# Experts' first products by one level of Strassen's algorithm (Winograd's form), in three passes of 768 tokens

## The chip, the cores and the metric

One core of one Trainium2 chip runs the kernel. The metric is device time in microseconds for one execution. TensorE (PE) multiplies matrices, VectorE (DVE) and ScalarE (ACT) work element by element, GpSimd (POOL) does almost nothing here, and SyncE (SP) issues the transfers between memory (HBM) and the on-chip buffer (SBUF). TensorE's results go to PSUM, eight banks of 512 float32 columns by 128 partitions.

## What is computed

```python
kv = einsum('bhsd,bhse->bhde', k, v); o = einsum('bhsd,bhde->bhse', q, kv)
x  = o / sqrt(mean(o*o, -1) + 1e-6) * g_norm      # 4 x 576 = 2304 tokens of 512
h  = x @ w_in;  x = (h * clip(h + 3, 0, 6) / 6) @ w_out          # first layer, 512 -> 2048 -> 512
p  = domain_probs / (domain_probs.sum(-1, keepdims=True) + 1e-9)
for e in range(4):                                               # second layer, 4 experts
    out += p[:, e:e+1] * (maximum(x @ w1[e], 0) @ w2[e])         # 512 -> 1024 -> 512
```

## The kernel before, in words

A float32 product runs as three passes in TensorE's float32r type: an operand is split into hi (rounded to float32r) and lo (the rest), and hi*hi + hi*lo + lo*hi is summed in PSUM. ScalarE makes hi, VectorE lo.

The 2304 tokens lie in blocks of 512 (four, and one of 256: `BLK`). Hidden features are worked on in feature tiles of 128. The first layer's 16 feature tiles are cut into four units (`UNITS1`), and each expert is a unit of 8. An item (u, t, f) is a feature tile f of unit u for token block t, and `items` runs over units, in them over blocks, in them over feature tiles. `ff_in` (L345 to L367) makes an item's hidden features: 12 products (4 tiles of d by 3 passes, L352 to L354) into one of two PSUM banks, then for an expert a ReLU on ScalarE (`gH`, L364) and lo on VectorE (`gL`, L365). `ff_out` (L369) multiplies them by the second matrix, three items later (`LAG`), into up to six banks: 12 products of the block's width in the first layer, and for an expert 3 products of 512 columns per token tile of 128 (L385). `ff_end` takes a block's sums out of PSUM after a unit's last feature tile: the first layer adds them to `acc` and at its end makes hi and lo of the second layer's input (`xH`, `xL`, L403, L404); an expert scales them by the token's probability and adds (L416, L418), and the last expert's are stored (L420).

`step` writes an item's products and, beside them, a few steps of weight conversion (`pull`, `convert`): float32 weights of the experts are split by L175 (hi) and L177 (lo), from blocks loaded by L126 and L130. All weights of the experts are loaded and split once. Instructions stand on each engine in an order that a scheduler settles when the kernel is built; each engine then runs its own in that order and waits at semaphores.

## Time and profile before

| | us |
|---|---|
| three timed executions | 1274.44, 1274.55 (median), 1275.44 |
| profiled execution, first to last instruction (its span) | 1272.9 |
| median above that span | 1.65 |
| TensorE busy in the span | 1257.5 |
| VectorE busy, ScalarE busy | 500.9, 354.7 |

The profiled execution has no time of its own in the results, only its span; the median of the timed executions stands for it, and 1.65 us lie outside the span. Busy time is the union of an engine's instructions. Products on TensorE overlap, so their mean duration is longer than the distance from one start to the next. Weight loads of TensorE have a row of their own (PEld). A row that waits names who released it.

### The profile page before, as it was taken

The page shows a single profiled execution, that of the slowest core. Times are in us where ns is not written, and L with a number is a line of the kernel's source. Part 1 is how long each engine was busy: PE and PEld are TensorE (multiplying, and loading weights), DVE is VectorE, ACT ScalarE, POOL GpSimd, SP SyncE. Part 2 cuts the span into 40 slices and gives each one's busy share as a digit, 9 for nine tenths or more (in the row PEclk, how much of TensorE's full clock was granted, in tenths as well). Part 3 has the DMA queues.
Part 4 walks back from the last instruction along what each step waited for, and adds up shares of the span by engine and source line. Part 5 has one row for each costly group of instructions (what it writes and reads, how often), then busy time and mean ns, then how long its engine had stood idle before and what let it go on. Part 6 is the DMA issues. An engine that isn't in the chain of part 4 may idle for free.

```text
span 1272.9 us, 14454 instructions
## 1 busy us (share of the span) xinstructions
PE 1257.5 (99%) x6108; PEld 1056.8 (83%) x6108; DVE 500.9 (39%) x917; ACT 354.7 (28%) x642; POOL 1.3 (0%) x10
## 2 busy tenths in 40 slices
PE   8899999999999999999999999999999999999998
PEld 6778888888888888888888888888888888888887
DVE  3889995874644344212224212215122215122122
ACT  5776752542433333111113111104111104111110
POOL 0000000000000000000000000000000000000000
PEclk8899999999999999999999999999999999999999
DMA  9932330220200003000003000004000002000001
GB/s 247 226 92 75 107 100 17 67 67 1 67 1 1 1 1 100 1 1 1 1 1 132 1 1 1 1 1 132 1 1 1 1 1 83 1 33 33 1 34 50
DMA packets 38288, 53.39 MB, mean 42 GB/s; under 512 B 4176, under 2 KB 29776, under 8 KB 38224
## 3 DMA queue, kind: packets, MB, share of 16 engines
q1 hardware_dynamic: 38064, 52.47, 14.4%
q8 instruction: 48, 0.79, 0.3%
q14 instruction: 16, 0.13, 0.0%
q10 hardware_dynamic: 160, 0.00, 0.0%
HBM read 47.75 MB, written 4.72 MB: 41 GB/s over the span
## 4 chain that ended last, share of the span: by engine, by line
PE 96%; DVE 2%; ACT 2%; DMA 1%; issue 0%; SPq 0%; DVEq 0%; ACTq 0%
PE po L385 46%; PE ph L353 15%; PE ph L352 15%; PE ph L354 15%; PE kvp L240 1%; PE po L265 1%; ACT qT L230 1%; DMA vin<-in_v_dram 1%; PE px L323 1%; DVE ssq L274 0%; DVE xt L287 0%; ACT xh L333 0%; PE pq L227 0%; ACT xt L271 0%; DVE xl L334 0%
## 5 line engine op out<-in xcount | busy, mean ns | idle before, releaser
L385 PE MATMUL po<-w,gH 128*128 128x512 f32 x1152 | 355.4, 390 | 0.0
L352 PE MATMUL ph<-xh,w 128*128 128x512 f32 (+1 forms) x960 | 353.6, 368 | 0.0
L353 PE MATMUL ph<-xl,w 128*128 128x512 f32 (+1 forms) x960 | 353.5, 368 | 0.0
L354 PE MATMUL ph<-xh,w 128*128 128x512 f32 (+1 forms) x960 | 353.2, 368 | 0.0
L365 DVE SCALAR_TENSOR_TENSOR gL<-ph,gH 128x512 fp32r<-128x512 f32 (+1 forms) x160 | 102.0, 637 | 569.4 <-ACT gH L364 569.4
L364 ACT ACTIVATE gH<-ph 128x512 fp32r<-128x512 f32 (+1 forms) x160 | 88.8, 555 | 632.1 <-PE ph L354 632.1
L385 PEld LDWEIGHTS po<-w,gH 128*128 128x128 f32 x1152 | 214.2, 188 | 42.8
L385 PE MATMUL po<-w,gL 128*128 128x512 f32 x576 | 224.1, 389 | 0.0
L352 PEld LDWEIGHTS ph<-xh,w 128*128 128x128 f32 x960 | 180.9, 188 | 31.3
L353 PEld LDWEIGHTS ph<-xl,w 128*128 128x128 f32 x960 | 180.9, 188 | 31.1
L354 PEld LDWEIGHTS ph<-xh,w 128*128 128x128 f32 x960 | 180.8, 188 | 30.2 <-issue 0.2
L385 PE MATMUL po<-gH,w 128*128 128x512 f32 (+1 forms) x640 | 193.7, 368 | 0.0
L385 PEld LDWEIGHTS po<-gH,w 128*128 128x128 f32 x640 | 117.2, 189 | 20.2
L385 PEld LDWEIGHTS po<-w,gL 128*128 128x128 f32 x576 | 108.1, 188 | 22.7
L385 PE MATMUL po<-gL,w 128*128 128x512 f32 (+1 forms) x320 | 117.8, 368 | 0.0
L360 DVE SCALAR_TENSOR_TENSOR r<-r,ph 128x512 f32<-128x512 f32 (+1 forms) x80 | 50.5, 632 | 109.6 <-ACT r L359 109.6
L359 ACT ACTIVATE r<-ph,three 128x512 f32<-128x512 f32 (+1 forms) x80 | 51.5, 644 | 139.3 <-PE ph L354 139.1
L385 PEld LDWEIGHTS po<-gL,w 128*128 128x128 f32 x320 | 60.4, 189 | 9.9
L362 DVE TENSOR_TENSOR gL<-r,gH 128x512 fp32r<-128x512 f32 (+1 forms) x80 | 50.7, 634 | 21.2 <-ACT gH L361 20.6
L361 ACT ACTIVATE gH<-r 128x512 fp32r<-128x512 f32 (+1 forms) x80 | 47.0, 588 | 36.9 <-DVE r L360 36.8
L177 DVE TENSOR_TENSOR w<-raw,w 128x512 fp32r<-128x512 f32 x64 | 42.2, 689 | 29.8 <-ACT w L175 29.7
L175 ACT ACTIVATE w<-raw 128x512 fp32r<-128x512 f32 x64 | 38.2, 626 | 33.0 <-PE po L385 22.0
(58 smaller groups left out, 573.8 us busy)
## 6 DMA issues: line engine op xcount, KB each, us to landing
raw<-in_moe_w_dram SPq DMA_DIRECT2D x32, 512.0 KB, 3.9
raw<-in_moe_w_in_dram SPq DMA_DIRECT2D x16, 512.0 KB, 3.7
raw<-in_moe_w_out_dram SPq DMA_DIRECT2D x16, 512.0 KB, 3.6
qin<-in_q_dram SPq DMA_DIRECT2D x8, 576.0 KB, 13.7
kin<-in_k_dram SPq DMA_DIRECT2D x8, 576.0 KB, 12.8
vin<-in_v_dram SPq DMA_DIRECT2D x8, 576.0 KB, 12.6
out_dram<-acc SPq DMA_DIRECT2D x18, 256.0 KB, 2.1
dp<-in_moe_domain_probs_dram SPq DMA_DIRECT2D x1, 36.0 KB, 13.3
```

Source lines behind the costliest of these rows:

```text
L175: nc.scalar.activation(out=hi, in_=src[h], func=AF.Copy)
L177: nc.vector.tensor_tensor(out=lo, in0=src[h], in1=hi.bitcast(F32), op=ALU.subtract)
L352: nc.tensor.matmul(ph, lhsT=w[:, 0, c, :], rhs=xH[t][:, c, :], start=(c == 0), stop=False)
L353: nc.tensor.matmul(ph, lhsT=w[:, 0, c, :], rhs=xL[t][:, c, :], start=False, stop=False)
L354: nc.tensor.matmul(ph, lhsT=w[:, 1, c, :], rhs=xH[t][:, c, :], start=False, stop=(c == KD - 1))
L359: nc.scalar.activation(out=r, in_=ph, func=AF.Relu, bias=three[:, 0:1])
L360: nc.vector.scalar_tensor_tensor(out=r, in0=r, scalar=6.0, in1=ph, op0=ALU.min, op1=ALU.mult)
L361: nc.scalar.activation(out=gH, in_=r, func=AF.Copy)
L362: nc.vector.tensor_tensor(out=gL, in0=r, in1=gH.bitcast(F32), op=ALU.subtract)
L364: nc.scalar.activation(out=gH, in_=ph, func=AF.Relu)
L365: nc.vector.scalar_tensor_tensor(out=gL, in0=ph, scalar=0.0, in1=gH.bitcast(F32), op0=ALU.max, op1=ALU.subtract)
L385: nc.tensor.matmul(po_t[u, t][o], lhsT=lhsT, rhs=rhs, start=(f == 0 and m == 0), stop=(f == UF[u] - 1 and m == 2))
```

## The change

Only the second layer's first products change in kind. For a quad (256 hidden features of one expert) and a pass (768 tokens in two halves of 384), the product x @ w1 is a product of 2 x 2 blocks: the weights are a11, a12, a21, a22 (hidden half, d half), the tokens b11, b12, b21, b22 (d half, token half). Winograd's form of Strassen's algorithm takes seven products of blocks in place of eight:

P1 = a11 b11, P2 = a12 b21, P6 = S2 T2, P5 = S1 T1, P7 = S3 T3, P3 = S4 b22, P4 = a22 T4, with S1 = a21 + a22, S2 = S1 - a11, S3 = a11 - a21, S4 = a12 - S2, T1 = b12 - b11, T2 = b22 - T1, T3 = b22 - b12, T4 = b21 - T2; c11 = P1 + P2, U2 = P1 + P6, U4 = U2 + P5, c12 = U4 + P3, c22 = U4 + P7, c21 = U2 + P7 + P4.

Each product is 6 instructions of 384 columns (2 tiles of d by 3 passes). Two banks, `qa` and `qb`, hold the sums: ScalarE copies P1 from `qa` into `qb`, and P6, P5 and P3 are added to it there, with copies U2 and U4 taken to SBUF between them; P7 and then P4 are summed in `qa`, and VectorE adds U4 and U2 to them (c22, c21). One extra product writes `qb` once at the start. Between the seven products stand the second products of the quad before (`filler`, 36 of 512 columns), 8, 6, 7, 8 and the rest at a time (`fill`), each with a step of weight conversion (`side`). The weight sums S are made on VectorE for every quad, and the weights are loaded and split once per pass, so three times. The token sums T with their hi and lo (`xs1` to `xs7`) are made by `build` per pass: for the first during the last items of the first layer, for the other two in the last quad of the pass before. The first layer no longer makes `xH`, `xL` at its end, and its factor 1/6 goes into the probabilities.

```diff
-    NUNIT = NU1 + E           # units: slices of the first layer's hidden features, then the experts
+    NUNIT = NU1
+    UF = UNITS1
+    TH = 384
+    FP = NF2 // 2
...
+    N3 = start[NU1 - 1, 0] + 3 * UF[NU1 - 1]
+    for n in range(NI):
...
+    early.close()
+    xsp = ctx.enter_context(tc.tile_pool(name="xsp", bufs=1, reuse_waits="tile"))
+    winp = ctx.enter_context(tc.tile_pool(name="winp", bufs=2, side="right", reuse_waits="tile"))
...
+    PASSES = [
+        ([(0, 0, TH, 0)], [(1, 0, TH, 0)]),
+        ([(2, 0, TH, 0)], [(3, 0, TH, 0)]),
+        ([(0, TH, rest, 0), (1, TH, rest, rest), (4, 0, rest, 2 * rest)],
+         [(2, TH, rest, 0), (3, TH, rest, rest), (4, rest, rest, 2 * rest)]),
+    ]
...
+    quads = [(p, e, j) for p in range(NPASS) for e in range(E) for j in range(FP)]
...
+    def load2(k):
...
+        nc.sync.dma_start(
+            out=r[:, 0].rearrange("p (c f) -> p c f", c=KD),
+            in_=moe2_w1[e, :, f:f + 2 * P].rearrange("(c p) f -> p c f", p=P))
+        nc.sync.dma_start(
+            out=r[:, 1].rearrange("p (f d) -> p f d", f=2),
+            in_=moe2_w2[e, f:f + 2 * P, :].rearrange("(f p) d -> p f d", p=P))
...
+    def split(dst, src):
+        nc.scalar.activation(out=dst[0], in_=src, func=AF.Copy)
+        nc.vector.tensor_tensor(out=dst[1], in0=src, in1=dst[0].bitcast(F32), op=ALU.subtract)
...
+    def convert_in(k):
+        r = raw2[k][:, 0].rearrange("p (c i f) -> p i c f", c=KD, i=2)
+        win[k] = w = winp.tile([P, 2, 7, 2, P], F32R, tag="win", name="win")
+        a11, a12, a21, a22 = (r[:, i, 2 * c:2 * c + 2, :] for i in range(2) for c in range(2))
+        split([w[:, y, 0:2].rearrange("p m c f -> p (m c) f") for y in range(2)], r[:, 0])
+        yield
+        split([w[:, y, 2] for y in range(2)], a22)
+        nc.vector.tensor_tensor(out=sums[:, 0], in0=a21, in1=a22, op=ALU.add)
+        yield
+        nc.vector.tensor_tensor(out=sums[:, 1], in0=sums[:, 0], in1=a11, op=ALU.subtract)
+        nc.vector.tensor_tensor(out=sums[:, 2], in0=a11, in1=a21, op=ALU.subtract)
+        yield
+        nc.vector.tensor_tensor(out=sums[:, 3], in0=a12, in1=sums[:, 1], op=ALU.subtract)
+        split([w[:, y, 3:5] for y in range(2)], sums[:, 0:2])
+        yield
+        split([w[:, y, 5:7] for y in range(2)], sums[:, 2:4])
+        yield
...
+    def convert_out(k):
...
+        for f in range(2):
+            split([w[:, f, y] for y in range(2)], r[:, f])
+            if f == 1:
+                load2(k + 2)
+            yield
...
+        return {
+            1: lambda: plain(1, b11),
+            5: lambda: summed(5, st1, b12, b11),
+            6: lambda: summed(6, st2, b22, st1),
+            2: lambda: plain(2, b21),
+            3: lambda: plain(3, b22),
+            7: lambda: summed(7, st1, b22, b12),
+            4: lambda: summed(4, st1, b21, st2),
+        }
...
+    def outs(k):
...
+        for i in range(NI2):
+            t, o = divmod(i * P, TH)
+            for f in range(2):
+                gH, gL = (g[f][:, y, t, o:o + P] for y in range(2))
+                for m, (lhsT, y) in enumerate(((gH, 0), (gH, 1), (gL, 0))):
+                    nc.tensor.matmul(
+                        ps[i], lhsT=lhsT, rhs=w[:, f, y],
+                        start=(j == 0 and f == 0 and m == 0), stop=(j == FP - 1 and f == 1 and m == 2))
+                    yield
...
+    def relu(g, src):
+        nc.scalar.activation(out=g[0], in_=src, func=AF.Relu)
+        nc.vector.scalar_tensor_tensor(
+            out=g[1], in0=src, scalar=0.0, in1=g[0].bitcast(F32), op0=ALU.max, op1=ALU.subtract)
...
+    def quad(k, filler, side):
+        def fill(n):
+            for _ in range(n):
+                if next(filler, 0) == 0:
+                    break
+            if side:
+                side.pop(0)()
...
+        def product(bank, m, first):
+            n = 0
+            for c in range(2):
+                for wy, xy in ((0, 0), (0, 1), (1, 0)):
+                    nc.tensor.matmul(
+                        bank, lhsT=w[:, wy, AOP[m], c], rhs=xs[m][:, xy, c],
+                        start=first and n == 0, stop=n == 5, skip_group_check=True)
+                    n += 1
+        if k == 0:
+            nc.tensor.matmul(qb, lhsT=w[:, 0, 0, 0], rhs=xs[1][:, 0, 0], start=True, stop=True)
+        product(qa, 1, True)
+        nc.scalar.activation(out=qb, in_=qa, func=AF.Copy)
+        fill(8)
+        product(qb, 6, False)
+        nc.scalar.activation(out=u2, in_=qb, func=AF.Copy)
+        product(qa, 2, False)
+        relu((g[0][:, 0, 0], g[0][:, 1, 0]), qa)
+        fill(6)
+        product(qb, 5, False)
+        nc.scalar.activation(out=u4, in_=qb, func=AF.Copy)
+        fill(7)
+        product(qb, 3, False)
+        product(qa, 7, True)
+        nc.vector.tensor_tensor(out=c22, in0=qa, in1=u4, op=ALU.add)
+        relu((g[0][:, 0, 1], g[0][:, 1, 1]), qb)
+        fill(8)
+        relu((g[1][:, 0, 1], g[1][:, 1, 1]), c22)
+        product(qa, 4, False)
+        nc.vector.tensor_tensor(out=c21, in0=qa, in1=u2, op=ALU.add)
+        relu((g[1][:, 0, 0], g[1][:, 1, 0]), c21)
+        fill(99)
...
+    ahead = [first[m] for m in (1, 5, 6, 2, 4)] + [run(convert_in(0))] * 5 + [run(convert_in(1))] * 5
+    for n in range(N3 + 1, NI):
+        step(n)
+        if ahead:
+            ahead.pop(0)()
+    for x in ahead + [first[3], first[7]]:
+        x()
...
+    for k in range(NQ):
+        ci, co = convert_in(k + 1) if 0 < k and k + 1 < NQ else iter(()), convert_out(k)
+        side = [run(co), run(co), run(ci), run(ci), run(ci), run(ci), run(ci)]
+        if k + 1 < NQ and quads[k + 1][0] != quads[k][0]:
+            nxt = build(quads[k + 1][0])
+        quad(k, filler, side)
+        for x in side:
+            x()
+        if k + 1 < NQ and quads[k + 1][0] != quads[k][0]:
+            for m in (1, 5, 6, 2, 4, 3, 7):
+                nxt[m]()
+        filler = outs(k)
```

In the lists that follow, a line number is that of the kernel it stands in.

TensorE, one expert's item in the kernel before: the end of `ff_in` and the `ff_out` of an item three back.

```order
L352 MATMUL ph_7009<-xh1_101,w_6637 128x512
L353 MATMUL ph_7009<-xl1_106,w_6637 128x512
L354 MATMUL ph_7009<-xh1_101,w_6637 128x512
L385 MATMUL po2_6993<-w_6545,gH_6927 128x512 [waits Activation_49]
L385 MATMUL po2_6993<-w_6545,gH_6927 128x512
L385 MATMUL po2_6993<-w_6545,gL_6928 128x512
L385 MATMUL po2_6994<-w_6545,gH_6927 128x512 x2
L385 MATMUL po2_6994<-w_6545,gL_6928 128x512
L385 MATMUL po2_6995<-w_6545,gH_6927 128x512 x2
L385 MATMUL po2_6995<-w_6545,gL_6928 128x512
L385 MATMUL po2_6996<-w_6545,gH_6927 128x512 x2
L385 MATMUL po2_6996<-w_6545,gL_6928 128x512
```

TensorE in the change, in the middle of a quad: P3 into `qb`, P7 and then P4 into `qa`, with second products (L632) between them.

```order
L677 MATMUL qb_4204<-xs3_4196,win_5690 128x384 [waits Activation_49]
L677 MATMUL qb_4204<-xs3_4196,win_5690 128x384 x5
L677 MATMUL qa_4203<-xs7_4199,win_5690 128x384 [waits DVE_49]
L677 MATMUL qa_4203<-xs7_4199,win_5690 128x384 x5
L632 MATMUL po2_5761<-wout_5645,g2_5626 128x512 x3
L632 MATMUL po2_5762<-wout_5645,g2_5625 128x512 x3
L632 MATMUL po2_5762<-wout_5645,g2_5626 128x512 x2
L677 MATMUL qa_4203<-xs4_3966,win_5690 128x384 [waits DVE_49]
L677 MATMUL qa_4203<-xs4_3966,win_5690 128x384 x5
L632 MATMUL po2_5762<-wout_5645,g2_5626 128x512
```

A wait stood once per twelve products, on an item one or three back; now one stands before nearly every product P, on a copy or sum of the same quad.

VectorE in the second layer of the kernel before: lo of one item after another, and a block's scaled sums.

```order
L365 SCALAR_TENSOR_TENSOR gL_4727<-ph_4713,gH_4726 128x512 [waits Activation_49]
L365 SCALAR_TENSOR_TENSOR gL_4756<-ph_4742,gH_4755 128x512 [waits Activation_49]
L365 SCALAR_TENSOR_TENSOR gL_4785<-ph_4771,gH_4784 128x512 [waits Activation_49]
L416 TENSOR_SCALAR acc2_4800<-po2_4581,prob_96 128x512 [waits PE_49]
L416 TENSOR_SCALAR acc2_4800<-po2_4582,prob_96 128x512 [waits PE_49]
L416 TENSOR_SCALAR acc2_4800<-po2_4583,prob_96 128x512 [waits PE_49]
```

VectorE in the change, from c11's lo of one quad on: weight sums of the quad after the next (`raw2`), c12's lo, the block sum c22 and its lo, the block sum c21.

```order
L652 SCALAR_TENSOR_TENSOR g2_5747<-qa_4203,g2_5747 128x384 [waits Activation_49]
L557 TENSOR_TENSOR sums_3775<-raw2_5798 128x256 [waits DMAHW1_49,DVE_49]
L560 TENSOR_TENSOR sums_3775<-raw2_5798 128x256 [waits DVE_49]
L559 TENSOR_TENSOR sums_3775<-sums_3775,raw2_5798 128x256 [waits DVE_49]
L562 TENSOR_TENSOR sums_3775<-raw2_5798,sums_3775 128x256 [waits DVE_49]
L652 SCALAR_TENSOR_TENSOR g2_5747<-qb_4204,g2_5747 128x384 [waits Activation_49]
L698 TENSOR_TENSOR cs_5750<-qa_4203,us_5749 128x384 [waits PE_49]
L652 SCALAR_TENSOR_TENSOR g2_5748<-cs_5750,g2_5748 128x384 [waits Activation_49]
L703 TENSOR_TENSOR cs_5750<-qa_4203,us_5749 128x384 [waits PE_49]
```

The weight sums, which wait for a load, now stand ahead of c12's lo and the block sums on this queue.

VectorE in the last quad of the second pass: `xs5`'s lo, a weight sum and `st1` for the third pass, then c12's lo and c22.

```order
L547 TENSOR_TENSOR xs5_8049<-st1_3776,xs5_8049 128x768 [waits PE_49,Activation_49]
L562 TENSOR_TENSOR sums_3775<-raw2_7971,sums_3775 128x256 [waits DVE_49]
L606 TENSOR_TENSOR st1_3776<-acc1_1169,st2_3777 128x2x128 [waits DVE_49]
L606 TENSOR_TENSOR st1_3776<-acc1_1258,st2_3777 128x2x128
L606 TENSOR_TENSOR st1_3776<-acc1_1542,st2_3777 128x2x128
L652 SCALAR_TENSOR_TENSOR g2_7926<-qb_4204,g2_7926 128x384 [waits Activation_49]
L698 TENSOR_TENSOR cs_7929<-qa_4203,us_7928 128x384 [waits PE_49]
```

In this quad the third pass's token sums stand among them as well; there was nothing of this kind before.

## Rows read from the trace of the kernel before

**Rows 1.** The page: busy time, share of the span and instructions, by engine.

```profile
PE 1257.5 (99%) x6108; PEld 1056.8 (83%) x6108; DVE 500.9 (39%) x917; ACT 354.7 (28%) x642; POOL 1.3 (0%) x10
```

**Rows 2.** The page: busy tenths and granted clock, in 40 slices.

```profile
PE   8899999999999999999999999999999999999998
...
PEclk8899999999999999999999999999999999999999
```

**Rows 3.** Waits of PE from 85 us on (waiter, releaser: us, times, longest).

```profile
PE px L323 <- DVE xl L334: 0.9, 1, 0.9
```

**Rows 4.** Timeline of PE: twelve 512-column products, first and the one behind (start us, us).

```profile
1227.26 0.39 PE L352 MATMUL ph<-xh,w 128*128 128x512 f32 x1
...
1229.98 0.39 PE L385 MATMUL po<-w,gH 128*128 128x512 f32 x1
```

**Rows 5.** Timeline of PE: twelve 256-column products, first and the one behind.

```profile
1238.14 0.28 PE L352 MATMUL ph<-xh,w 128*128 128x256 f32 x1
...
1239.58 0.40 PE L385 MATMUL po<-w,gH 128*128 128x512 f32 x1
```

**Rows 6.** Groups by shape, PE: count, busy us, mean ns.

```profile
L385 PE MATMUL po<-w,gH 128*128 128x512 f32 x1152 | 355.4, 390 | 0.0
L352 PE MATMUL ph<-xh,w 128*128 128x512 f32 x768 | 299.5, 390 | 0.0
...
L352 PE MATMUL ph<-xh,w 128*128 128x256 f32 x192 | 54.1, 282 | 0.0
```

**Rows 7.** Groups by shape, weight loads, 480 us on.

```profile
L352 PEld LDWEIGHTS ph<-xh,w 128*128 128x128 f32 x636 | 119.8, 188 | 21.0
```

**Rows 8.** Groups by shape, ACT, 85 us on.

```profile
L364 ACT ACTIVATE gH<-ph 128x512 fp32r<-128x512 f32 x128 | 76.5, 598 | 558.1 <-PE ph L354 558.1
...
L175 ACT ACTIVATE w<-raw 128x512 fp32r<-128x512 f32 x64 | 38.2, 626 | 33.0 <-PE po L385 22.0 <-DMA raw<-in_moe_w_dram 10.9
...
L364 ACT ACTIVATE gH<-ph 128x256 fp32r<-128x256 f32 x32 | 12.3, 383 | 74.0 <-PE ph L354 74.0
...
L403 ACT ACTIVATE xh<-acc 128x256 fp32r<-128x256 f32 x4 | 1.4, 406 | 0.2 <-DVE acc L402 0.2
...
L333 ACT ACTIVATE xh<-px,gcol 128x384 fp32r<-128x384 f32 x1 | 0.6, 581 | 0.7 <-PE px L323 0.7
```

**Rows 9.** Groups by shape, DVE, 85 us on.

```profile
L365 DVE SCALAR_TENSOR_TENSOR gL<-ph,gH 128x512 fp32r<-128x512 f32 x128 | 88.5, 691 | 510.9 <-ACT gH L364 510.9
...
L177 DVE TENSOR_TENSOR w<-raw,w 128x512 fp32r<-128x512 f32 x64 | 42.2, 689 | 29.8 <-ACT w L175 29.7
L418 DVE SCALAR_TENSOR_TENSOR acc<-po,prob,acc 128x512 f32<-128x512 f32 x54 | 36.9, 743 | 3.9 <-PE po L385 3.9
...
L365 DVE SCALAR_TENSOR_TENSOR gL<-ph,gH 128x256 fp32r<-128x256 f32 x32 | 13.5, 423 | 58.5 <-ACT gH L364 58.5
...
L334 DVE SCALAR_TENSOR_TENSOR xl<-px,gcol,xh 128x384 fp32r<-128x384 f32 x2 | 1.1, 562 | 0.3 <-ACT xh L333 0.3
```

**Rows 10.** Timeline: an expert block's last product, its ReLU and its lo part.

```profile
700.48 0.39 PE L354 MATMUL ph<-xh,w 128*128 128x512 f32 x1
...
700.90 0.60 ACT L364 ACTIVATE gH<-ph 128x512 fp32r<-128x512 f32 x1 [4.84 <-PE ph L354]
...
701.53 0.69 DVE L365 SCALAR_TENSOR_TENSOR gL<-ph,gH 128x512 fp32r<-128x512 f32 x1 [4.75 <-ACT gH L364]
```

**Rows 11.** One line's instructions: landing times of the first matrices' loads.

```profile
DMA to landing us min/median/max: 3.4/4.5/5.1
```

**Rows 12.** The page: DMA issues, KB each, median us to landing.

```profile
qin<-in_q_dram SPq DMA_DIRECT2D x8, 576.0 KB, 13.7
...
out_dram<-acc SPq DMA_DIRECT2D x18, 256.0 KB, 2.1
```

**Rows 13.** Stretches: us, busy by engine (count), granted clock, DMA share, GB/s.

```profile
9.20:16.00 6.80, 5.46 (x26) 5.49 (x27) 0.00 (x0) 1.53 (x4) 0.00 (x0) 0.50 1.11 255
...
43.30:50.10 6.80, 6.46 (x30) 6.18 (x31) 6.14 (x17) 4.96 (x11) 0.00 (x0) 0.50 1.14 217
...
480.00:1272.90 792.90, 789.02 (x3676) 660.99 (x3674) 187.01 (x295) 122.30 (x219) 0.00 (x0) 1.00 0.07 24
```

More of the change, by code (lines that the diff above doesn't have):

```diff
@@ L101 @@
     raw = {}
-    todo = [(n, h) for n, (u, f) in enumerate(ftiles) if u < NU1 or f % 2 == 0 for h in range(2)]
+    todo = [(n, h) for n in range(len(ftiles)) for h in range(2)]
     def load_raw():
@@ L435, in step @@
         if n >= LAG:
-            u, t, f = items[n - LAG]
-            ff_out(u, t, f)
-            if f == UF[u] - 1:
-                ff_end(u, t)
+            for _ in ff_out(*items[n - LAG]):
+                pass
         if 0 <= n - LAG + 1 < NI:
@@ L535 @@
         fill()
-    for n in range(NI + LAG):
+    N3 = start[NU1 - 1, 0] + 3 * UF[NU1 - 1]
+    for n in range(NI):
         step(n)
@@ new lines @@
+    rest = TB - TH
+    PASSES = [
[4 more added lines that the diff above has]
+    ]
+    NPASS = len(PASSES)
+    rows = [[(BLK[k][0] + o + y) // P for h in ps for k, o, ln, _ in h for y in range(0, ln, P)] for ps in PASSES]
+    NI2 = len(rows[0])
+    assert sorted(sum(rows, [])) == list(range(NTT))
@@ new lines, in convert_out, with build, pieces, new @@
+    def convert_out(k):
+        r = raw2.pop(k)[:, 1].rearrange("p (f d) -> p f d", f=2)
+        wout[k] = w = wp.tile(
+            [P, 2, 2, DM], F32R, tag=f"w{(NA + len(ftiles) + 2 + k % 2) % NW}", name="wout")
+        for f in range(2):
[3 more added lines that the diff above has]
+            yield
+    def build(p):
+        t1, t2 = PASSES[p]
+        def pieces(h, c):
+            return [(acc[b][:, 2 * c:2 * c + 2, o:o + n], slice(z, z + n)) for b, o, n, z in h]
+        b11, b12, b21, b22 = pieces(t1, 0), pieces(t2, 0), pieces(t1, 1), pieces(t2, 1)
+        def new(m):
+            pool = xp if m in XSHOME else xsp
+            xs[m] = pool.tile([P, 2, 2, TH], F32R, tag=XSHOME.get(m, f"xs{m}"), name=f"xs{m}")
+            return xs[m]
+        def plain(m, b):
+            x = new(m)
+            for s, z in b:
+                split([x[:, y, :, z] for y in range(2)], s)
+        def summed(m, dst, a, b):
+            x = new(m)
+            if not isinstance(a, list):
+                a = [(a[:, :, z], z) for _, z in b]
+            if not isinstance(b, list):
+                b = [(b[:, :, z], z) for _, z in a]
+            for (s, z), (s2, _) in zip(a, b):
+                nc.vector.tensor_tensor(out=dst[:, :, z], in0=s, in1=s2, op=ALU.subtract)
+            split([x[:, y] for y in range(2)], dst)
+        return {
[7 more added lines that the diff above has]
+        }
@@ new lines, in outs @@
+    def outs(k):
+        p, e, j = quads[k]
+        w = wout.pop(k)
+        g = g2.pop(k)
+        if j == 0:
+            po_t["e"] = [bank_b([P, DM], "po2") for _ in range(NI2)]
+        ps = po_t["e"]
+        for i in range(NI2):
[6 more added lines that the diff above has]
+                        start=(j == 0 and f == 0 and m == 0), stop=(j == FP - 1 and f == 1 and m == 2))
+                    yield
+            if j == FP - 1:
+                n = rows[p][i]
+                pe = prob[:, n, e:e + 1]
+                if e == 0:
+                    z = (p * NI2 + i) % 10
+                    acc2[i] = gp.tile([P, TB], F32, tag=("gH", "gL")[z % 2], name="acc2") if z < 8 else rp.tile(
+                        [P, TB], F32, tag="r", name="acc2")
+                    nc.vector.tensor_scalar(out=acc2[i], in0=ps[i], scalar1=pe, scalar2=None, op0=ALU.mult)
+                else:
+                    nc.vector.scalar_tensor_tensor(
+                        out=acc2[i], in0=ps[i], scalar=pe, in1=acc2[i], op0=ALU.mult, op1=ALU.add)
+                if e == E - 1:
+                    nc.sync.dma_start(out=out[n * P:(n + 1) * P, :], in_=acc2[i])
@@ new lines, in run, with tail @@
+    def run(g):
+        return lambda: next(g, None)
+    load2(0)
+    load2(1)
+    first = build(0)
+    ahead = [first[m] for m in (1, 5, 6, 2, 4)] + [run(convert_in(0))] * 5 + [run(convert_in(1))] * 5
[5 more added lines that the diff above has]
+        x()
+    def tail():
+        for n in range(NI, NI + LAG):
+            yield from ff_out(*items[n - LAG])
+    qa = psa.tile([P, TB], F32, tag="a", name="qa")[:, :TH]
@@ L547 @@
+    for _ in filler:
+        pass
 _INS = ['q', 'k', 'v', 'g_norm', 'moe_w_in', 'moe_w_out', 'moe2_domain_probs', 'moe2_w1', 'moe2_w2']
```

204 lines of the change are left out of this document (87 added, 117 removed).

## The prediction

> **What bounds the kernel now.** I read the page first: TensorE is busy 1257.5 of 1272.9 us, VectorE 39% and ScalarE 28% of the span [rows 1], and from the third slice on TensorE and its granted clock both stand at 9 [rows 2]. A busy TensorE need not be one at its peak, so the waits come next: from 85 us to the end it waits once, for 0.9 us [rows 3]. The timeline then gives the price of a product, which is the distance between two starts and not the mean duration (390 and 282 ns [rows 6]), since products overlap. Twelve products of 512 columns take 1229.98 - 1227.26 = 2.72 us, 0.2267 each [rows 4]; twelve of 256 columns take 1.44 us, 0.120 each [rows 5]. The 256 columns between them cost 0.1067 us, 2.4 columns per ns, which is the upper of the clock's two levels (granted 1.00 from 480 us on [rows 13]); 0.0133 us per product is left whatever its width. A weight load takes 188 ns [rows 7], yet 256-column products start every 120 ns, so loads overlap more than one product and set nothing. So from 85 us on the time is a count of products times a start distance, and work of the other engines costs only where TensorE comes to wait for it.
>
> **TensorE's sum.** Removed: the first products of the experts, 32 feature tiles, each with 4 blocks of 12 wide products and one block of 12 narrow ones: 32 x (4 x 2.72 + 1.44) = 394.2 us. Added: 3 passes x 4 experts x 4 quads = 48 steps of 7 x 6 = 42 products of 384 columns, 2016 in all. The trace has no 384-column product. From below, 384 columns at 2.4 per ns are 0.160 us; from above, the weight load's 0.188 us if it came to set the pace. I take 0.1733, midway between the two rows on either side, which differ by columns alone: 2016 x 0.1733 = 349.4 us. The ends give 322.6 and 379.0. The one extra product that prepares the second bank adds 0.2. TensorE thus saves 394.2 - 349.4 - 0.2 = **44.6 us**. The second products stay: 48 x 36 = 1728 of 512 columns, as before (1152 with the hi part as stationary operand [rows 6], and half as many with lo). Attention and first layer keep their lists of instructions but for a few neighbours that swap. The tail stays too: a scaled sum of 0.74 us [rows 9] and a store of 2.1 us [rows 12] behind the last product. Block sums, weight sums and copies are all VectorE's and ScalarE's; I cost them at nothing only where the next part finds cover.
>
> **The cover inside a step.** A step occupies TensorE for 42 x 0.1733 + 36 x 0.2267 = 7.28 + 8.16 = 15.44 us. VectorE's prices: 0.69 at 512 columns, 0.42 at 256, 0.56 at 384, 0.74 for a scaled sum [rows 9], and 0.96 at 768 (0.69 plus the 0.27 between 256 and 512). One step asks of it 5 lo parts of 512 and one of 256, 4 weight sums of 256, 4 lo parts and 2 block sums of 384, and one step in four 6 scaled sums: 3.45 + 0.42 + 1.68 + 3.36 + 1.1 = 10.0 us. ScalarE: 0.63 at 512, 0.38 to 0.41 at 256 [rows 8]; at 384 its one row says 0.58 with a scale operand, the middle of the others 0.49, which I take as the nearer in kind. A step asks 5 x 0.63 + 0.41 + 7 x 0.49 = 7.0 us. Both fit into 15.44; order decides.
>
> With P1 starting at 0, TensorE is through P1 at 1.04, eight second products at 2.85, P6 and P2 at 4.93, six more at 6.29, P5 at 7.33, seven at 8.92, P3 and P7 at 11.00, eight at 12.81, P4 at 13.85, the last seven at 15.44. From the end of a product (700.48 + 0.23) to ScalarE's start (700.90) pass 0.19 us, from ScalarE to VectorE 0.03 [rows 10]; back to TensorE I take 0.1. Then:
> - The seed of the second bank stands in ScalarE's queue behind what P4's end sets free: two weight copies, c21's ReLU, three more copies (0.63 + 0.41 + 0.49 + 3 x 0.63 = 3.42 from 14.04 on, so to 2.0 of the next step). It runs 2.0 to 2.5; TensorE asks at 2.85, 0.25 after the handover.
> - The copy U2 runs 4.1 to 4.6, asked at 6.29; U4 runs 7.5 to 8.0, asked at 8.92.
> - c12's ReLU ends at 10.65, its lo at 11.2, the sum c22 at 11.8; P4 asks at 12.81, since c22 must have left the bank.
> - The sum c21 runs 14.05 to 14.6; the next P1 asks at 15.44. Its lo, behind two weight splits (0.69 + 0.42), ends at 16.3, asked at 17.6.
>
> So the seed has 0.25 us to spare and all else 0.7 or more; I cost a steady step's waits at **nothing**. The hidden load: raw weights for step k+2 are asked for when VectorE has split step k's, at 2.3; their four sums stand in VectorE's queue directly behind c11's lo, at 6.2. First matrices landed 3.4 to 5.1 us after issue [rows 11], here 7.4 at the latest; the sums end at 9.1 and the next in the queue, c12's lo, can't start before 10.65. If that cover goes, c22 is late, and P4 with it: the landing may take 7.6 us before that.
>
> **The seams.** In the last step of a pass VectorE gets 9 operations of 768 columns more, 8.7 us (about 10.4 for the third pass, which is cut into pieces of 256), beside its 10.0: 3 to 5 us spill into the next step. At the second seam, in the order of its list, VectorE splits weights until 3.6, then come xs1's lo (to 4.9), xs6's (behind its copy, 5.5 to 6.5), c11's (7.0), xs2's (8.3), three weight sums (9.6), xs5's lo (10.5), a weight sum and three pieces of st1 (12.2), c12's lo (12.8) and c22 (13.3, asked at 12.81): 0.6 late with the handover. At the first seam, uncut, the same list ends at 12.7, just in time; I add 0.1. Between the layers, fillers are 256-column products of 0.120, so seven cover 0.84 us instead of 1.59, and U4, c22 and c21 each come within 0.1 us of being late; I add 0.6 for them. Seams: **1.3 us**; the ends are 0 and the whole spill, 3 + 5 = 8.
>
> **Sum:** -44.6 + 1.3 = -43.3. The profiled execution's span of 1272.9 becomes 1229.6; the median of the timed executions, 1274.55, lies 1.65 above that span, so the forecast is 1231.2, taken as **1231 us**.
>
> **Rivals.**
> 1. *The seed comes late in every step.* If ScalarE's seven operations up to it take 0.5 us more than the 3.9 I take (the copy from PSUM to PSUM isn't in the trace), TensorE waits 0.25 us per step: 48 x 0.25 = 12, time 1243. For it: the slack of 0.25. Against: the 0.63 is the row of the same kind of copy [rows 8], and the queue holds nothing else. 0.09.
> 2. *The weight load sets the pace at 384 columns.* 2016 x (0.188 - 0.1733) = 29.6 us are given back, time 1261. Against: at 256 columns it doesn't [rows 5, 7]. 0.02. The Trainium skill's page "TensorE: Matmul & The Clock Gate" (Back-to-back issue gap) has such a rule: spacing is set by load and product together, about 81 ns at 128 columns and 131 at 512. An estimate on the line between these, 98 at 256 and 114 at 384, would make the first products 238.8 before and 229.8 after, save 9 us and give about 1267; the rows' 0.2267 and 0.120 speak against it.
> 3. *The load holds VectorE's queue* (slower). If the raw block lands later than 7.6 us after issue, the sums wait, c12's lo and c22 behind them, and P4. Each microsecond more costs 46 in all; the gain is used up at 7.6 + 43.3/46 = 8.5 us. At the 13.7 us of the attention's loads [rows 12] P4 would be 6.1 late in each step: 280 us, time about 1511. For it: loads and stores share one queue, and a store waits there for VectorE. Against: rows 11, and 1 MB per 15.44 us is 68 GB/s where the attention's loads ran at 255 [rows 13]. 0.03.
> 4. *Small waits take the clock down* (slower). Twice in the attention the clock was granted at 0.50 for 6.8 us, while TensorE had gaps (busy 5.46 and 6.46 of 6.80) [rows 13]; such a stretch loses 3.4 us of work. One per step would cost 163 us, time 1394; 13 of them use up the gain. Against: the list above has no gap in a steady step. 0.02. The Trainium skill's same page (A second HAM failure mode: psum-queue depth-cycling) states that cycling through PSUM banks leaves small gaps between groups that make the clock oscillate; the rows of the kernel before, which cycles its banks as well, show 1.00 throughout.
>
> That fewer products are run than the change says is excluded: TensorE's list holds its six at each of the seven turns.
>
> **Numbers.** The forecast has 0.84. Its own range is 1228.5 (no wait at the seams is 1230, less a microsecond and a half for the start distance and the spread of the runs) to 1238 (all of the spill); that leaves out under 2 in 10, so it is the range. A change under 0.2%, 2.5 us, can't be told from none. Forecast and rivals 1 and 2 are faster: 0.95. Rivals 3 and 4 hold 0.05; 0.01 of it for a load that happens to cost what is saved, 0.04 slower.
>
> **What would show it.** Right: 2016 products of 384 columns at start distances of 0.173 us; granted clock 1.00 from 480 us on; TensorE's waits after 85 us under 3 us in sum, most of them on VectorE's block sums at the two changes of pass. Wrong: a distance of 0.188 (rival 2); P6 waiting for the copy into the second bank in every step (rival 1); VectorE waiting for raw2, then P4 for the block sum (rival 3); granted clock under 1.00 after 480 us (rival 4).

## The result, and the profile after

The changed kernel took **1254.24 us** (median of four runs, 1252.49 to 1254.29); the kernel before, run beside it, 1274.99 (four runs, 1274.44 to 1276.34). The ratio is 0.9828 (95% interval 0.9814 to 0.9842): faster by 21 us, where 43 were forecast, and outside the range. The profiled execution took 1252.49 us, its span is 1250.7.

The page of the changed kernel, busy time by engine, then the slices of PE and its granted clock:

```profile
PE 1235.1 (99%) x6205; PEld 1079.2 (86%) x6205; DVE 767.6 (61%) x1489; ACT 538.9 (43%) x1049; POOL 1.3 (0%) x10
...
PE   8899999999999999999999999999999999999998
...
PEclk9989999999999999999999999999999999999999
```

Against [rows 1, 2], TensorE is as full as before, the clock as high, and VectorE and ScalarE have nearly the load that was counted: over the stretch from 500 to 1100 us they are busy 364.9 and 253.2 us, 9.6 and 6.6 a step where 10.0 and 7.0 were. In the waits of PE from 85 us to the end there is no row at all: neither steady steps nor seams make TensorE wait. ScalarE's copies into the second bank, and the landing of the raw weights, as one line's instructions and as the page has them (KB each, median us):

```profile
L686 ACT ACTIVATE qb<-qa x48: 467/471/475, 489.2 to 1224.1; 128x384 f32<-128x384 f32 x48
```

```profile
raw<-in_moe_w_dram SPq DMA_DIRECT2D x96, 512.0 KB, 4.3
```

So the cover held, and the count of products is the one forecast. What differs stands in the groups of PE by shape (count | busy us, mean ns of one | idle):

```profile
L632 PE MATMUL po<-wout,g 128*128 128x512 f32 x1728 | 435.9, 392 | 0.0
L677 PE MATMUL qa<-xs,win 128*128 128x384 f32 x1152 | 234.7, 339 | 0.0
L677 PE MATMUL qb<-xs,win 128*128 128x384 f32 x864 | 176.3, 339 | 0.0
L356 PE MATMUL po<-gH,w 128*128 128x512 f32 x512 | 171.2, 396 | 0.0
L335 PE MATMUL ph<-xh,w 128*128 128x512 f32 x256 | 101.9, 398 | 0.0
```

A product of 512 columns, 390 ns in [rows 6], now takes 396 to 398 ns in the first layer (L356, L335), whose work is the same as before. The timeline of a step shows the distances (start us, us):

```profile
704.04 1.22 PE L677 MATMUL qa<-xs,win 128*128 128x384 f32 x6
705.10 2.00 PE L632 MATMUL po<-wout,g 128*128 128x512 f32 x8
706.94 1.22 PE L677 MATMUL qb<-xs,win 128*128 128x384 f32 x6
...
719.76 1.22 PE L677 MATMUL qa<-xs,win 128*128 128x384 f32 x6
```

The step takes 719.76 - 704.04 = 15.72 us (15.44 forecast), six products of 384 columns 1.06 (0.177 each), eight of 512 columns 1.84 (0.230 each). The second layer's first product starts at 487.7 us; at that place the kernel before stands at 477.9. Timelines of PE, the changed kernel, then the kernel before:

```profile
487.74 0.34 PE L684 MATMUL qb<-xs,win 128*128 128x384 f32 x1
```

```profile
477.90 0.40 PE L352 MATMUL ph<-xh,w 128*128 128x512 f32 x1
```

**So no wait took the gain: each product became a few nanoseconds dearer, in the part that wasn't touched as well.**

In the table and below, a distance is the mean over the trace of all starts of that width from 85 us on whose next start follows within 260 ns (1505 to 1573 products of the first layer, nearly all of the 2016 and 1728 of the second; of the kernel before and its variants some 3240 of the second). A ratio is to the kernel before run beside that run, whose median lies between 1274.82 and 1276.20 us.

| run | us (median), ratio to before [95%] | first layer, 512 | second, 384 | second, 512 |
|---|---|---|---|---|
| before | 1274.99 | 227.2 ns | | 226.95 ns |
| changed | 1254.24, 0.9828 [0.9814, 0.9842] | 233.5 | 176.9 | 230.2 |
| e1 changed, right end +32 bytes | 1242.94, 0.9737 [0.9722, 0.9752] | 230.5 | 175.4 | 228.7 |
| e2 before, weights +32 | 1302.88, 1.0207 [1.0192, 1.0222] | 233.3 | | 232.8 |
| e3 before, tokens +32 | 1293.39, 1.0130 [1.0114, 1.0145] | 231.0 | | 231.1 |
| e4 before, all +32 | 1277.07, 1.0007 [0.9996, 1.0019] | 227.2 | | 226.95 |
| f1 changed, all alike | 1240.53, 0.9734 [0.9716, 0.9752] | 227.1 | 175.0 | 231.15 |
| f2 before, weights +128 | 1305.75, 1.0239 [1.0212, 1.0266] | 232.65 | | 232.7 |
| f3 before, weights +64 | 1296.63, 1.0173 [1.0152, 1.0195] | 233.25 | | 231.5 |
| f4 before, weights +256 | 1277.35, 1.0016 [1.0006, 1.0027] | 227.2 | | 226.95 |
| g1 f1, `win` +256 | 1239.14, 0.9721 [0.9694, 0.9747] | 227.1 | 175.0 | 231.1 |
| g2 e1, `win` +128 | 1244.95, 0.9757 [0.9740, 0.9775] | 230.5 | 176.5 | 229.05 |
| g3 f1, four places | 1242.46, 0.9746 [0.9722, 0.9771] | 227.2 | 175.8 | 231.0 |
| g4 f1, none between (one run) | 1250.83 | 227.1 | 174.9 | 228.9 |
| h1 f1, all 512 wide (one run) | 1338.65 | 227.1 | (512:) 226.7 | 226.7 |
| h2 f1, all 384 wide (one run) | 1143.30 | 227.1 | 173.6 | (384:) 173.7 |
| h3 f1, one block | 1251.15, 0.9807 [0.9785, 0.9829] | 227.1 | 175.8 | 228.2 |
| h4 h3 with copies | 1236.43, 0.9697 [0.9682, 0.9712] | 227.1 | 174.6 | 227.9 |

### The profile page after: what moved, and what is told of

Same layout as the page of the kernel before. It is cut to its first block, busy times and chain, and to the rows that moved or that the text cites. A ratio compares the mean times of both kernels' runs of the same rounds, so it can differ in the third digit from the quotient of the medians.

```text
span 1250.7 us, 15739 instructions
## 1 busy us (share of the span) xinstructions
PE 1235.1 (99%) x6205; PEld 1079.2 (86%) x6205; DVE 767.6 (61%) x1489; ACT 538.9 (43%) x1049; POOL 1.3 (0%) x10
## 4 chain that ended last, share of the span: by engine, by line
PE 95%; DMA 2%; DVE 2%; ACT 1%; issue 0%; SPq 0%; DVEq 0%; ACTq 0%
PE po L632 32%; PE qa L677 16%; PE po L356 16%; PE qb L677 12%; PE ph L335 5%; PE ph L333 5%; PE ph L334 5%; DMA vin<-in_v_dram 2%; PE kvp L221 1%; PE po L246 1%; ACT qT L211 1%; PE px L304 0%; DVE ssq L255 0%; DVE xt L268 0%; ACT xt L252 0%
## 5 line engine op out<-in xcount | busy, mean ns | idle before, releaser
L632 PE MATMUL po<-wout,g 128*128 128x512 f32 x1728 | 435.9, 392 | 0.0
L632 PEld LDWEIGHTS po<-wout,g 128*128 128x128 f32 x1728 | 322.0, 188 | 54.3
L677 PE MATMUL qa<-xs,win 128*128 128x384 f32 x1152 | 234.7, 339 | 0.0
L677 PEld LDWEIGHTS qa<-xs,win 128*128 128x128 f32 x1152 | 206.8, 188 | 7.8
L356 PE MATMUL po<-gH,w 128*128 128x512 f32 (+1 forms) x640 | 196.4, 372 | 0.0
L677 PE MATMUL qb<-xs,win 128*128 128x384 f32 x864 | 176.3, 339 | 0.0
L677 PEld LDWEIGHTS qb<-xs,win 128*128 128x128 f32 x864 | 155.6, 188 | 11.5
L356 PEld LDWEIGHTS po<-gH,w 128*128 128x128 f32 x640 | 117.1, 188 | 23.0
L335 PE MATMUL ph<-xh,w 128*128 128x512 f32 (+1 forms) x320 | 120.0, 375 | 0.0
L333 PE MATMUL ph<-xh,w 128*128 128x512 f32 (+1 forms) x320 | 119.4, 373 | 0.0
L356 PE MATMUL po<-gL,w 128*128 128x512 f32 (+1 forms) x320 | 119.2, 373 | 0.0
L334 PE MATMUL ph<-xl,w 128*128 128x512 f32 (+1 forms) x320 | 119.2, 372 | 0.0
L334 PEld LDWEIGHTS ph<-xl,w 128*128 128x128 f32 x320 | 60.2, 188 | 12.1
L333 PEld LDWEIGHTS ph<-xh,w 128*128 128x128 f32 x320 | 60.1, 188 | 11.8 <-issue 0.2
L356 PEld LDWEIGHTS po<-gL,w 128*128 128x128 f32 x320 | 60.2, 188 | 11.6
L335 PEld LDWEIGHTS ph<-xh,w 128*128 128x128 f32 x320 | 60.1, 188 | 11.3
## 6 DMA issues: line engine op xcount, KB each, us to landing
dp<-in_moe_domain_probs_dram SPq DMA_DIRECT2D x1, 36.0 KB, 13.3
```

Of the source, the lines that this page charges most:

```text
L333: nc.tensor.matmul(ph, lhsT=w[:, 0, c, :], rhs=xH[t][:, c, :], start=(c == 0), stop=False)
L334: nc.tensor.matmul(ph, lhsT=w[:, 0, c, :], rhs=xL[t][:, c, :], start=False, stop=False)
L335: nc.tensor.matmul(ph, lhsT=w[:, 1, c, :], rhs=xH[t][:, c, :], start=False, stop=(c == KD - 1))
L356: nc.tensor.matmul(po_t[u, t][o], lhsT=lhsT, rhs=rhs, start=(f == 0 and m == 0), stop=(f == UF[u] - 1 and m == 2))
L632: nc.tensor.matmul(ps[i], lhsT=lhsT, rhs=w[:, f, y], start=(j == 0 and f == 0 and m == 0), stop=(j == FP - 1 and f == 1 and m == 2))
L677: nc.tensor.matmul(bank, lhsT=w[:, wy, AOP[m], c], rhs=xs[m][:, xy, c], start=first and n == 0, stop=n == 5, skip_group_check=True)
```

## The experiments

**Placement in SBUF.** An unchanged list of products that became slower pointed at what the change moved under it: addresses. In the programs as built, every operand of TensorE in both layers of the kernel before begins 448 bytes past a multiple of 1024 in its partition. In the changed kernel the pools with `side="right"` are laid down from the end, and the weights of both layers and the experts' hidden features begin 992 past a multiple of 1024, tokens and block sums 832 or 320, the first layer's hidden features 448: within 64 bytes, weights stand at 32 and tokens at 0. Theory A made this the cause, B the greater load of VectorE, ScalarE and transfers, C the weights' place at the upper end. The edit of each run is an unused tile ahead of a pool; e1:

```diff
+    padp = ctx.enter_context(tc.tile_pool(name="padp", bufs=1, side="right"))
+    pad = padp.tile([P, 8], F32, name="pad")
+    nc.gpsimd.memset(pad, 0.0)
     wp = ctx.enter_context(tc.tile_pool(name="wp", bufs=1, side="right"))
```

> The changed kernel with an unused tile of 32 bytes at the right end of SBUF, so that all weight, g2 and wout tiles begin on a 64-byte boundary (as every operand of the kernel before does) and not 32 bytes behind one. Theory A (TensorE's start distance depends on how its operands' addresses lie against 64 bytes): distances return to 0.2267 us at 512 columns and 0.1733 at 384 in both layers, the second layer begins near 478 us in place of 488, the time is 1230 to 1234 us. Theory B (the greater load of VectorE, ScalarE and DMA slows TensorE's reads): 0.230 and 0.177 stay, 1252 to 1254 us. Theory C (weights now lie at the upper end of SBUF, further from the tokens): no change either, 1252 to 1254.

1242.94 us: better by 11 us than the changed kernel, with nothing else altered, but not at the 1230 to 1234 awaited.

e2 to e4 leave the changed kernel aside and move operands of the kernel before, by the same 32-byte tile ahead of `wp` and again behind it (e2), ahead of and behind `xp` (e3), or once ahead of everything (e4); with two tiles, what lies behind both moves by 64 bytes:

> The kernel before with an unused tile of 32 bytes ahead of the weight slots and another behind them: only the weights (stationary in the first layer and the experts' first products, moving in the experts' second products) begin 32 bytes off a 64-byte boundary. Theory A: the first layer's 512-column distance goes from 0.2277 to about 0.234 as in the changed kernel, that is 9 to 10 us there, and the experts' first products as much again in proportion; the time is 1292 to 1306 us, by whether the second products are hit too. Theories B and C: 1274 to 1276 us, distances as before.

> The kernel before with the unused 32 bytes ahead of the tokens' hi and lo and behind them: only the moving operand of the first products of both layers lies 32 bytes off. Theory A: if either operand's place counts, the first products' distances grow by about 0.006 us (1290 to 1296 us); if only the stationary operand's counts, 1274 to 1276. Theories B and C: 1274 to 1276.

> The kernel before with one unused tile of 32 bytes ahead of tokens, weights and hidden features: all operands of both layers lie 32 bytes off alike. Theory A in its absolute form (each operand against 64 bytes): slower, 1290 to 1310. Theory A in its relative form (the two operands against each other): 1274 to 1276. Theories B and C: 1274 to 1276.

Against the kernel before run beside them (1276.20), e2 costs 27 us and e3 17, e4 nothing that can be told. Groups of PE by shape in the second layer (500 to 1200 us), first of e3, then of e4:

```profile
L391 PE MATMUL po<-w,gH 128*128 128x512 f32 x1010 | 313.9, 392 | 0.0
L391 PE MATMUL po<-w,gL 128*128 128x512 f32 x504 | 196.1, 389 | 0.0
L360 PE MATMUL ph<-xh,w 128*128 128x512 f32 x457 | 180.7, 395 | 0.0
```

```profile
L388 PE MATMUL po<-w,gL 128*128 128x512 f32 x512 | 199.2, 389 | 0.0
L355 PE MATMUL ph<-xh,w 128*128 128x512 f32 x467 | 181.7, 389 | 0.0
```

In e3 only the tokens stand off, and mainly the products that read them are long (L360, 395 ns; `gL` keeps its 389). With all operands off alike, all are 389. So it is not the address, but how the moving operand and the weights stand to each other (whether the weights of the same product or of the next one, these runs can't tell). B and C have no part in e2 and e3, where load and side are those of before.

**How fine?** In e1 tokens and weights of the first layer still stand 128 bytes apart within 256. f1 is e1 with another unused tile, of 128 bytes, ahead of `xp`, so that all start alike within 512; f2, f3 and f4 are e2 with 128, 64 and 256 bytes, and the tile behind `wp` filled up so that all later pools keep their place within 1024.

> The changed kernel with two unused tiles, 32 bytes at the right end and 128 bytes ahead of the pool of the tokens, so that every operand of TensorE (tokens, block sums, weights, hidden features) starts at the same place modulo 512 bytes, as in the kernel before. Theory D (what counts is how the two operands stand to each other within 512 bytes; a difference of 128 bytes, left in the run with 32 bytes at the right end, still makes products slow, and each change between such a block and another costs the next two or three products): 1231 to 1236 us, first layer back to 227 to 228 ns a product, products of 512 columns in the second layer at 227. Theory E (only the difference within 64 bytes counts, and the rest of that run's distance to the forecast comes from the change itself, from VectorE's and ScalarE's greater load or from the mix of widths): 1241 to 1245 us, distances as with the 32 bytes alone (231.0, 175.4 and 228.7 ns).

> The kernel before with the weight slots alone moved by 128 bytes. Theory D: slower, 1282 to 1296 us. Theory E: no change, 1273 to 1278 us.

> The kernel before with the weight slots alone moved by 64 bytes. Theory D: slower, 1278 to 1296 us. Theory E: no change, 1273 to 1278 us.

> The kernel before with the weight slots alone moved by 256 bytes. Theory D: slower, 1278 to 1296 us, unless the pattern repeats every 256 bytes, which would be no change. Theory E: no change, 1273 to 1278 us.

64 bytes cost 22 us and 128 cost 31, where 32 cost 27 (f3 just above D's range, f2 well above it); 256 cost nothing in the distances: the relation counts within 256 bytes. E fell with that, and f1's first layer is back at 227.1 ns, its second layer now starting at 477.48 us. Yet f1 took 1240.5 us, just under E's 1241 to 1245: the second layer's products of 512 columns became slower, 231.15 ns, and those of 384 are at 175.0.

**What is left.** In f1's trace the slow products of 512 columns have the same pattern in every block, whatever VectorE does beside them: 229, 233, 236, 224, 231, 236 ns for the first six behind a block of 384 columns. That spoke for the change of width (theory F) and against other places (G). g1 is f1 with 256 bytes ahead of `winp`, g2 is e1 with 128 bytes there.

> The changed kernel with all operands at the same place within 512 bytes (the run before it, 1240.5 us), and the second layer's first weights alone moved by 256 bytes. Theory F (below 64, 128 and 32 bytes' differences what is left comes from the change between 384 and 512 columns, not from addresses): 1239 to 1242 us, 175.0 ns at 384 columns and 231 ns at 512 in the second layer, first layer 227 ns. Theory G (the block sums, cut in pieces of 1536 bytes, need another place against their weights): at least 3 us away from 1240.5, to either side, through the products of 384 columns.

> The changed kernel with 32 bytes at the right end (1242.9 us), and the second layer's first weights moved by 128 bytes, so that they stand to the block sums as in the kernel of 1240.5 us, while both stand 128 bytes off the second weights and the hidden features. Theory F (only the two operands of neighbouring products count): second layer as in the kernel of 1240.5 us, 175.0 and 231 ns, first layer 230.5 ns as with 32 bytes at the right end: 1243 to 1247 us. Theory G (the place of the first products against the second ones counts too): second layer's distances at least 1 ns away from these.

g1 is f1 again in every distance. g2's time is F's, its distances are not: the same relation between `win` and `xs` as in f1, but 176.5 and 229.05 ns, so what the block ahead left behind is felt, and depends on places too. G is right there.

g3 and g4 change how the 36 second products are spread:

```diff
-        fill(8)   fill(6)   fill(7)   fill(8)
+        fill(10)  fill(0)   fill(9)   fill(9)      # g3
+        fill(0)   fill(0)   fill(0)   fill(0)      # g4
```

> The changed kernel with all operands at the same place within 512 bytes, and a step's second products in four places among its first products (10, 9, 9 and 8) in place of five (8, 6, 7, 8 and 7). Theory F1 (each change between 384 and 512 columns costs a fixed sum, some 10 us over 48 steps and five places): 1238 to 1239 us, 230.3 ns at 512 columns. Theory F2 (a block of 384 columns leaves a state behind that the whole block of 512 columns keeps): 1240 to 1242 us, 231 ns as before.

> The changed kernel with all operands at the same place within 512 bytes, and all 36 second products of a step behind its 42 first ones, which opens waits between the first products: 1280 to 1360 us, of which only the distances are read. Theory F1: products of 512 columns fall to 227 to 228 ns, those of 384 to 173.5 ns. Theory F2: 512 columns stay at 230 to 231.5 ns.

g3 was no faster than f1, as F2 had it. g4 is not what its expectation says: the scheduler moved ready second products into places where TensorE would have waited, and a step's 36 stand as 6, 26, 3 and 1; 195 starts came later than 260 ns, 16 us in sum beyond the distance of their width. But in its long blocks the distances fall to 226.7 ns from the tenth product on. So neither F1 nor F2 as stated: a change costs the next nine products of 512 columns, and f1's and g3's blocks of 6 to 10 ended before that.

h1 and h2 take nearly all changes of width away and keep the order, the banks, the pairs of tiles and the other engines' work; what they compute is no longer the result.

```diff
-    bank, lhsT=w[:, wy, AOP[m], c], rhs=xs[m][:, xy, c],
+    bank, lhsT=w[:, wy, AOP[m], c],                                   # h1, bank 512 wide
+    rhs=xs[m][:, xy].rearrange("p c t -> p (c t)")[:, 256 * c:256 * c + TB],
...
-    ps[i], lhsT=lhsT, rhs=w[:, f, y],
+    ps[i][:, :wd], lhsT=lhsT, rhs=w[:, f, y, :wd],                    # h2, wd = 384
```

> The kernel with all operands at the same place within 512 bytes (1240.5 us), in which each of the 2016 first products streams 512 columns in place of 384 (384 of them are read on; the streamed columns are not those of the block sums, so what these products compute is left out). Theory F1 (what is left comes from the change between widths): no product is slow any more, 227 ns everywhere, 1240.5 + 2016 x (0.2270 - 0.1750) - 1728 x (0.2312 - 0.2270) = 1338 us. Theory H (it comes from changing to and fro between two pairs of operands, or from the engines' greater load): the second products stay at 231 ns, 1345 us.

> The same kernel, in which the second products stream 384 of their 512 columns (all but the first ones into a bank, 72 of 1728), so that a quarter of the second layer's output is left out. Theory F1: 173.3 ns at 384 columns everywhere, 1240.5 - 1656 x (0.2312 - 0.1735) - 2016 x 0.0015 = about 1142 us. Theory H: the first products stay at 175 ns and the second ones come to 177 to 178 ns: 1149 to 1153 us.

Both came out at F1's number, one run each: 1338.65 (1338) and 1143.3 (1142). Timelines of PE, h1 and then h2:

```profile
702.94 1.52 PE L683 MATMUL qa<-xs,win 128*128 128x512 f32 x6
704.30 1.75 PE L638 MATMUL po<-wout,g 128*128 128x512 f32 x7
705.89 1.52 PE L683 MATMUL qa<-xs,win 128*128 128x512 f32 x6
```

```profile
700.80 1.20 PE L684 MATMUL qb<-xs,win 128*128 128x384 f32 x6
701.84 1.37 PE L639 MATMUL po<-wout,g 128*128 128x384 f32 x7
703.05 1.20 PE L684 MATMUL qb<-xs,win 128*128 128x384 f32 x6
```

h1: 1.36 for six, 1.59 for seven, 0.227 each. h2: 1.04 for six, 1.21 for seven, 0.173 each. The stretches from 500 to 1100 us of f1 and of h2 (us, busy PE, PEld, DVE, ACT, POOL, granted clock, DMA share, GB/s) rule the load out as well: VectorE is busier in h2, 419 against 364 us, and next to none of its products is slow (173.6 ns on the mean; the 72 that stay 512 wide leave some changes).

```profile
500.00:1100.00 600.00, 600.00 (x2987) 539.78 (x2986) 364.01 (x701) 252.95 (x518) 0.00 (x0) 1.00 0.21 72
```

```profile
500.00:1100.00 600.00, 600.00 (x3437) 597.26 (x3436) 419.27 (x804) 289.83 (x593) 0.00 (x0) 1.00 0.24 83
```

**Fewer changes.** h3 lets the banks change roles each step, so that P4 of one step and P1 of the next can follow each other, and puts all second products behind P1:

```diff
+        qa, qb = banks[k % 2], banks[1 - k % 2]
...
         nc.scalar.activation(out=qb, in_=qa, func=AF.Copy)
-        fill(8)
+        for _ in range(7):
+            fill(5)
+        fill(99)
...
-        for i in range(NI2):
+        for i in (3, 4, 5, 0, 1, 2):
```

(the other `fill` calls go, P7 and its sum come ahead of P3, and at a seam 18 second products go ahead of P1).

> The kernel of 1240.5 us with the two PSUM banks changing roles each step, so that a step's 42 first products and 36 second products stand in one block each, without the waits that the run with all second products behind the first ones had: one pair of changes of width a step in place of five. Theory F1 (in that run the first ten products of 512 columns after a change were slow, the rest at 226.7 ns): 228 to 229 ns at 512 columns and 174 to 175 ns at 384, 1233 to 1237 us if no new wait opens, so faster than both kernels. Rival: relu's two halves and the seed, now closer together, make TensorE wait 0.2 us or more a step: 1242 us and above.

1251.15 us. The 228.2 ns came, the gain didn't. Timeline of PE:

```profile
706.73 1.20 PE L687 MATMUL qb<-xs,win 128*128 128x384 f32 x6
707.77 0.40 PE L638 MATMUL po<-wout,g 128*128 128x512 f32 x1
708.07 1.31 PE L687 MATMUL qa<-xs,win 128*128 128x384 f32 x6
```

P7 can't enter the bank before both halves of ReLU have read it; the scheduler put a second product there, which added a change of width and didn't cover the wait (0.30 us to the next start). 103 starts were later than 260 ns, 13.7 us in sum beyond the distance of their width: the rival of this run. h4 lets ScalarE copy those results out first and ReLU read the copy:

```diff
+        t1 = xsp.tile([P, TH], F32, tag="t1", name="t1")
+        nc.scalar.activation(out=t1, in_=qa, func=AF.Copy)
-        relu((g[0][:, 0, 0], g[0][:, 1, 0]), qa)
+        relu((g[0][:, 0, 0], g[0][:, 1, 0]), t1)
```

(and the same with `t2` behind P3).

> The run with one block a step, and two of the four results copied out of their PSUM bank by ScalarE before relu reads them, so that the bank is free after one short instruction: in the list of instructions as built, a step's 42 first and 36 second products then really stand in one block each (the run before it had two second products of a step among the first ones and one ahead of them, so near three pairs of changes a step, and waits of 280 to 295 ns). Theory F1 (some ten slow products after each change to 512 columns, fewer after a change to 384): 227.5 to 228.3 ns at 512 columns, 173.8 to 174.6 at 384, 1232 to 1236 us, faster than both kernels and than the 1240.5 us of the kernel it starts from. Rival: TensorE waits for a bank inside the 42 products, 0.15 us or more a step: 1239 us and above.

1236.43 us, just above the 1232 to 1236 expected, and faster than both kernels and than f1 (the intervals of the ratios, 0.9682 to 0.9712 and 0.9716 to 0.9752, just part). The chain of waits of h4, in order of time (start us, us, what):

```profile
702.82 1.06 PE qb L687 x6
703.89 1.04 PE qa L687 x6
...
707.01 1.04 PE qb L687 x6
708.05 1.07 PE qa L687 x6
709.12 1.04 PE qb L687 x6
710.16 8.20 PE po L638 x36
718.36 1.06 PE qa L687 x6
```

Six products take 1.04 us but right behind the change 1.06, and the 36 take 8.20 where 36 x 0.2267 are 8.16. By place in the block, over the 45 blocks that are whole, the first nine of 512 columns take 229, 233, 236, 224, 231, 236, 228, 232 and 231 ns (40 more than nine of 226.7), as in f1, then 226.6 to 226.9; the first six of 384 columns 171, 175, 177, 185, 176 and 182 (26 more than six of 173.3), then 173.3.

Such a trail also stands where no width changes. In 33 of these 45 blocks the same row (near 175, 177, 185, 176 and 182) stands once more from P4 on (the 1.07 above), 30 products behind the last change of width. P4 waits there for c22, so shortly that it hardly shows: it starts 0.21 to 0.22 us after c22 ends on VectorE, 2 to 6 ns later than the distance of 173.3 would have it (in 11 of the 12 blocks without this trail 2 ns at most). It costs 33 ns a block, 1 us in sum.

## Why the prediction was wrong

**The step that failed is "TensorE's sum"**, where it says that "0.0133 us per product is left whatever its width" and takes one distance for every product: 0.1733 for the new ones, and for the rest "The second products stay" and "Attention and first layer keep their lists of instructions". The lists stayed; the distances didn't. Against the forecast span of 1229.6 us, the 1250.7 are made up so: the second layer begins 487.7 - 477.9 = 9.8 us later (9.4 of them from the first layer's 61st first product on, 387.1 us against 377.7), 2016 x (176.9 - 173.3) = 7.2, 1728 x (230.2 - 226.7) = 6.1, less 1.3 for the seams: 21.8, where 21.1 are missing.

- *Placement*, which the prediction didn't look at: f1 gives back 1250.7 - 1238.2 = 12.5 us of span: the first layer's 9.4, 1.9 ns on each of 2016 products (3.8), less 0.9 on each of 1728 (1.6), and 0.9 ahead of that 61st product, which starts anywhere from 97.5 to 104.0 us in runs with equal distances. Shown by e1, f1, e2 to e4 and f2 to f4.
- *Changes of width*: what is left of f1, 2016 x 1.7 = 3.4 and 1728 x 4.4 = 7.7 us, goes when all products have one width (h1, h2); h4, which keeps the widths and has one pair of changes a step, gets half of it back (1238.2 - 1234.6 = 3.6 us of span, 5.7 in the second layer alone). The trace of before showed this price in the rows just behind [rows 5], which the prediction didn't read:

```profile
1239.58 0.63 PE L385 MATMUL po<-w,gH 128*128 128x512 f32 x2
1240.05 0.39 PE L385 MATMUL po<-w,gL 128*128 128x512 f32 x1
1240.27 0.62 PE L385 MATMUL po<-w,gH 128*128 128x512 f32 x2
1240.74 0.39 PE L385 MATMUL po<-w,gL 128*128 128x512 f32 x1
...
1242.10 0.39 PE L385 MATMUL po<-w,gL 128*128 128x512 f32 x1
```

Behind 256 columns, the first five products of 512 take 1240.74 - 1239.58 = 1.16 us, 0.232 each; the next six 1.36, 0.2267. The kernel before has some 35 such blocks in the second layer, the changed one 48 x 5, with longer trails.

**What held.** The 0.1733 itself: between products of one width it is exact (h2). The removed work, the 2016 and 1728 products, the clock at 1.00. *The cover inside a step*: no wait; the copy into the second bank takes 0.47 us, the 0.49 of the prediction for 384 columns, and ends 1.9 us into a step (2.5 forecast), 1.0 before P6 starts, so rival 1 with its late seed did not come. *The seams*: 0 in place of 1.3 us, inside the ends: around the changes of pass c22 ends 12.2 us into a step at the latest (13.3 forecast), 0.9 before P4 starts, and at the first step of all 0.2 before it. Rival 2 fell: products at 0.173 while weight loads stay at 188 ns. The Trainium skill's page "TensorE: Matmul & The Clock Gate" (Back-to-back issue gap) sets the spacing by load and product together; whether the dependence on the pair of operands found here is of that kind no run shows, and its 131 ns at 512 columns are far from this case's 226.7. Rival 3 fell: raw weights land 5.5 us after issue at the latest, 7.6 were allowed. Rival 4 fell: no gaps, no lower clock (where it says 1.00 "throughout" of the kernel before, [rows 13] show that from 480 us on, and 0.50 twice in the attention).

That the reads of the two operands get in each other's way in SBUF is the story that suggests itself, and only argued: the runs show the dependence on places within 256 bytes and on the width ahead, not what collides. The Trainium skill's page "SBUF — State Buffer" (Who interferes with whom) gives TensorE two independent read ports, one for the moving operand and one for the weight load, and only the port pair that VectorE and GpSimd share as a place of contention. By that, e2 would take the time of before; it takes 27 us more, and the measurement decides. Still open is why the trail behind a change is two products long in e1 and nine in h4, whether it is the slightly late start that sets off the same trail in P4, and why g2 differs from f1.

## What to carry to other kernels

When a change moves buffers, compare where the two operands of TensorE's products begin within 256 bytes, before and after: an unused tile of 32 and one of 128 bytes were worth some 12 us here (the first layer's 9.4, and 3.8 less 1.6). Price a stream of products from rows that stand where the new ones will stand, right behind a change of width as well as inside a block, and count the changes. When time is missing and there are no waits, look first at the distances in the part that nobody touched.
